# Paired rows of w_out per descriptor, gate and value weights read with a column step of two

## The chip, the cores and the metric

The kernel runs on one core of one Trainium2 chip. The metric is device time in microseconds of one execution. Before the change its median over 7 runs is 797.02 us (796.52 to 797.72).

## The reference

A light convolution over the sequence is followed by a gated feed-forward block. `x` is 8 x 4096 x 192, `weight` is 8 heads x 7 taps, `w_gate` and `w_val` are 192 x 1536 and `w_out` is 1536 x 192.

```
w = softmax(weight, axis=-1)                       # per head, 7 taps
x_pad = 6 zero rows ahead of each sequence
conv[b, s, h, :] = sum_k w[h, k] * x_pad[b, s + k, h, :]     # 24 columns a head
t = conv.reshape(32768, 192)
g = t @ w_gate;  v = t @ w_val
out = (g * sigmoid(g) * v) @ w_out                 # float32
```

## The kernel before

The 32768 tokens are cut into 64 blocks of 512 tokens. For each block the 1536 hidden columns are cut into 12 chunks of 128, so the main loop has 768 steps; step `n` is block `n // 12`, chunk `n % 12`. TensorE holds 192 = 3 x 64 input columns as three slices of 64 rows: the rows 0 to 63 of the array work on the gate and the rows 64 to 127 on the value, so one pair of matmuls (64 rows x 128 columns, 512 tokens) runs side by side. A step is three such pairs (L530), then ScalarE's Silu of the gate (L539) and VectorE's product with the value (L541), which gives `h` as 128 hidden columns x 512 tokens. `gate` and `val` have three PSUM banks each.

The hidden columns come from `w16`, the two weight matrices side by side in SBUF: 128 partitions x 3 x 1536, fp16. The stationary operand of chunk `j` is 128 neighbouring columns of it. The partition of `h` is therefore the hidden column within the chunk, and `wo16[p, j, :]` has to hold the row of `w_out` that belongs to it.

The down-projections (`slot`, `down`, L556) are put between the steps, four slots a block, each of 12 to 36 matmuls of 64 rows x 192 columns, in pairs again. Which slot stands behind which step is written out by hand in the loop from L645 on. For the first block it has its own numbers (slots at n = 9, 11, 13); from the second block on the slots stand at j = 1, 4, 7, 10. `after` is the Silu whose end a slot waits for.

The convolution is a product with a band matrix, made on the chip. Its taps are normalised (softmax), split into two fp16 numbers (`split`), brought onto the partitions by two matmuls (`tapbank`, L279), spread along 16 columns (`spread`, L290) and multiplied with shifted unit matrices (`shift`, L234) into `taps` (L310), four pieces of 16 columns. Four copies make `wide` of them (L323). The first four blocks are convolved on their own path: `early(e)` multiplies `wide` with the windows `xe[e]` of x (L365), casts it into `tme` (L383), and, for the blocks 0 to 2, `eturn` transposes it on TensorE (L423) with the unit matrix `ident` (L331) and copies it into `xc` (L428). The block 3 goes through memory (`eout`, `efetch`). From the second unit of four blocks on, `conv_half` does the same with larger windows in `x16`, and its result goes through memory and a transposing transfer.

Each engine works in the order in which the instructions are written (`seq`). GpSimd's queue issues all loads that change the type: `xe`, `w16` (`load_w`, three transfers a piece, in pieces of 384, 640 and 512 columns), `wo16` (`load_wo`, two halves), then the later `xe` and `x16`. Between them stand its iotas: `pid` and `jn` at the head, `cid` (L194) behind the third piece of `w16`. `ident` compares `cid` with `pf`. `keep_warm` gives TensorE matmuls on zeros ahead of the taps' products, so that it isn't idle there: seven of 512 columns, and, behind the products into `tapbank`, five of 128.

Of the kernel before, what the change touches and what calls it, by code (L numbers as in the profile page):

```python
# [10 lines left out]
def kernel(  # L11
# [9 lines left out]
    nc = tc.nc  # L21
    fp32 = mybir.dt.float32
    fp16 = mybir.dt.float16
    i32 = mybir.dt.int32
# [10 lines left out]
    P = 128  # L35
# [78 lines left out]
    def xe_load(e):  # L114
        for r, (g0, g1) in enumerate(ER):
            w0, w1 = 2 * g0, 2 * g1
            if e == 0 and r == 0:
                windows(xe[e], 0, 0, EO, 1, w1)
                windows(xe[e], 0, 0, EO, 0, 1, i0=pad, i1=Q - 2)
            else:  # L120
                windows(xe[e], Q * r, e * TB, EO, w0, w1, at=w0)

# [47 lines left out]
    def load_wo(c0, c1):  # L170
        seq(
            nc.gpsimd.dma_start(
                out=wo16[:, c0:c1, :],
                in_=moe_w_out[P * c0 : P * c1, :].rearrange("(c p) d -> p c d", p=P),
            )
        )

# [2 lines left out]

    pid = small("pid", [P, 1], i32)
    seq(nc.gpsimd.iota(pid, pattern=[[0, 1]], base=0, channel_multiplier=1))
    jn = small("jn", [P, 4, Q], i32)
    seq(nc.gpsimd.iota(jn, pattern=[[-16, 4], [1, Q]], base=0, channel_multiplier=0))  # L184
    xe_tile(0)
    seq(nc.vector.memset(xe[0][0:Q, 0, :], 0.0))
    xe_load(0)
    load_w(0, 384)
    load_w(384, 1024)
    xe_tile(1)  # L190
    xe_load(1)
    load_w(1024, Dff)
    cid = small("cid", [P, P], i32)
    seq(nc.gpsimd.iota(cid, pattern=[[1, P]], base=0, channel_multiplier=0))  # L194
    load_wo(0, 6)
    load_wo(6, NCH)
    xe_tile(2)
# [4 lines left out]
    for r in range(2):  # L202
        for low in (0, 32):
            load_x(1, r, low=low)

    pq_i = small("pq_i", [P, 1], i32)
    seq(nc.vector.tensor_single_scalar(pq_i, pid, 15, op=ALU.bitwise_and))
    pq = small("pq", [P, 1])
    seq(nc.vector.tensor_copy(pq, pq_i))
    pk = small("pk", [P, 1])  # L210
    seq(nc.vector.tensor_tensor(pk, pid, pq, op=ALU.subtract))
    eye = small("eye", [P, 16], fp16)
    seq(
        nc.vector.tensor_scalar(
            eye, jn[:, 0, 0:16], scalar1=pq, scalar2=None, op0=ALU.is_equal
        )
    )
    eyes = small("eyes", [P, 16, 2 * H], fp16)
    seq(nc.scalar.copy(eyes, eye.unsqueeze(2).to_broadcast([P, 16, 2 * H])))
    both = small("both", [P, 1])  # L220
    seq(
        nc.vector.scalar_tensor_tensor(
            both, pk, 1.0 / 16, pq, op0=ALU.mult, op1=ALU.add
        )
    )
    wexp = small("wexp", [H, K + 1])
    seq(nc.vector.memset(wexp[:, K : K + 1], 1e-9))
    split = small("split", [H, 2, K + 1, 16], fp16)
    seq(nc.vector.memset(split[:, :, K, :], 0.0))
    shift = small("shift", [P, 4, 2, Q], fp16)  # L230

    def make_shift(n):
        seq(
            nc.vector.tensor_tensor(  # L234
                shift[:, n : n + 2],
                jn[:, n : n + 2].unsqueeze(2).to_broadcast([P, 2, 2, Q]),
                both.unsqueeze(2).unsqueeze(3).to_broadcast([P, 2, 2, Q]),
                op=ALU.is_equal,
            )
        )  # L240

    make_shift(0)

    wmax = small("wmax", [H, 1])
    seq(nc.vector.tensor_reduce(wmax, wraw, axis=AX.X, op=ALU.max, negate=True))
    seq(nc.scalar.activation(wexp[:, 0:K], wraw, AF.Exp, bias=wmax))
    warmed = small("warmed", [P, 1], fp16)
    seq(nc.scalar.activation(warmed, fill[:, 0:1], AF.Silu))
    make_shift(2)
    wsum = small("wsum", [H, 1])  # L250
    seq(nc.vector.tensor_reduce(wsum, wexp, axis=AX.X, op=ALU.add))
    seq(nc.vector.reciprocal(wsum, wsum))
    wide_exp = wexp[:, 0:K].unsqueeze(2).to_broadcast([H, K, 16])
    seq(
        nc.vector.tensor_tensor(
            split[:, 0, 0:K],
            wide_exp,
            wsum.unsqueeze(2).to_broadcast([H, K, 16]),
            op=ALU.mult,
        )  # L260
    )
    seq(
        nc.vector.scalar_tensor_tensor(
            split[:, 1, 0:K],
            wide_exp,
            wsum,
            split[:, 0, 0:K],
            op0=ALU.mult,
            op1=ALU.subtract,
        )  # L270
    )
    tap = small("tap", [P, 2 * H], fp16)
    spread = small("spread", [P, 16, 2, H], fp16)

    def spread_taps():
        bank = apool.tile([P, TB], fp32, tag="acc0", name="tapbank")
        for a in range(2):
            seq(
                nc.tensor.matmul(  # L279
                    bank[:, a * H : a * H + H],  # L280
                    split[:, a].rearrange("h k q -> h (k q)"),
                    eye[0:H, 0:H],
                    start=(a == 0),
                    stop=True,
                    skip_group_check=True,
                )
            )
        seq(nc.vector.tensor_copy(tap, bank[:, 0 : 2 * H]))
        seq(
            nc.vector.tensor_tensor(  # L290
                spread.rearrange("p j a h -> p j (a h)"),
                eyes,
                tap.unsqueeze(1).to_broadcast([P, 16, 2 * H]),
                op=ALU.mult,
            )
        )

    wide = small("wide", [P, 2, H, Q], fp16)
    band = small("band", [P, H, 32], fp16)
# [3 lines left out]
    def make_wide():  # L303
        banks = [
            ppool.tile([P, TB], fp32, tag=tag, name="taps") for tag in ("gate", "val")
        ]
        for n in range(4):
            c0 = 16 * 2 * H * (n % 2)
            seq(
                nc.tensor.matmul(  # L310
                    banks[n // 2][:, c0 : c0 + 16 * 2 * H],
                    shift[:, n].rearrange("p r i -> p (r i)"),
                    spread.rearrange("p j a h -> p (j a h)"),
                    start=(n % 2 == 0),
                    stop=True,
                    skip_group_check=True,
                )
            )
        seq(nc.vector.tensor_copy(pf, pid))
        for h0 in (0, 4):  # L320
            for n in range(2):
                seq(
                    (nc.scalar.copy, nc.vector.tensor_copy)[n](  # L323
                        wide[:, :, h0 : h0 + 4, 32 * n : 32 * n + 32],
                        banks[n].rearrange("p (j a h) -> p a h j", a=2, h=H)[
                            :, :, h0 : h0 + 4, :
                        ],
                    )
                )
        seq(  # L330
            nc.vector.tensor_scalar(  # L331
                ident, cid, scalar1=pf, scalar2=None, op0=ALU.is_equal
            )
        )

# [186 lines left out]
    def gate_val(n):  # L522
        b, j = divmod(n, NCH)
        g = ppool.tile([P, TB], fp32, tag="gate", name="gate")
        v = ppool.tile([P, TB], fp32, tag="val", name="val")
        for k in range(SL):
            for half, o in ((0, g), (1, v)):
                p0 = Q * half
                seq(
                    nc.tensor.matmul(  # L530
                        o,
                        w16[p0 : p0 + Q, k, ts(j, P)],
                        xc[b][k][p0 : p0 + Q, 0:TB],
                        start=(k == 0),
                        stop=(k == SL - 1),
                    )
                )
        sg = hpool.tile([P, TB], fp16, tag="sig", name="sig", bufs=3)
        silu[n] = seq(nc.scalar.activation(sg, g, AF.Silu)).ins  # L539
        hj = hpool.tile([P, TB], fp16, tag="h", name="h", bufs=15)  # L540
        seq(nc.vector.tensor_tensor(hj, sg, v, op=ALU.mult))  # L541
        hbuf[n] = hj
# [79 lines left out]

    warm = ppool.tile([P, TB], fp32, tag="gate", name="warm")

    def keep_warm(count, width=TB):
        for _ in range(count):
            seq(
                nc.tensor.matmul(  # L628
                    warm[:, 0:width], fill[:, 0:P], fill[:, 0:width],
                    start=True, stop=True, skip_group_check=True,  # L630
                )
            )

# [1 line left out]
    acc_banks = (apool, "acc0"), (apool, "acc1")  # L635
    keep_warm(7)
    spread_taps()
    keep_warm(5, P)
    make_wide()
    early(0, (gate_bank, gate_bank, val_bank))  # L640
    eturn(0, (*acc_banks, gate_bank))
# [3 lines left out]
    for n in range(n_steps):  # L645
        b, j = divmod(n, NCH)
        u, ls = divmod(n, ustep)
        work = None
        if n in (11, 19):

            def work(e=2 if n == 11 else 3):
                early(e, (gate_bank, gate_bank, val_bank))

        at = (28, 31) if u == 0 else (10, 22)
# [3 lines left out]
                conv_half(u + 1, hh)  # L658

        gate_val(n)  # L660
        if n == 5:
            early(1, (*acc_banks, gate_bank))
        elif n == 7:
            eturn(1, (*acc_banks, gate_bank))
        elif n in (9, 11):
            slot(1 if n == 9 else 2, b, silu[n - 1], work)
        elif n == 13:
            slot(3, 0, silu[n - 1])
        elif j % 3 == 1 and b:
            k = {1: 3, 4: 4, 7: 1, 10: 2}[j]  # L670
            slot(k, b - 1 if j < 7 else b, silu[n - 2], work if j > 4 else None)
            if j == 4 and work:
                work()
        if n == 18:
            eturn(2, (*acc_banks, gate_bank))
        elif n == 20:
            eout(3)
        elif n == 21:
            efetch(3)
        if u + 1 < NU:  # L680
            if ls == at[0]:
                conv_dup(u + 1)
# [59 lines left out]
```

## Time and profile before

| | before |
|---|---|
| median of 7 runs | 797.02 us (796.52 to 797.72) |
| the profiled execution's own time | 797.6 us |
| its span in the profile | 795.8 us |
| TensorE matmuls busy | 785.1 us (99%) |
| VectorE busy | 583.1 us (73%) |
| ScalarE busy | 522.0 us (66%) |
| gate and value matmuls (L530) | 4608 of 377 ns, their loads 94 ns |
| down-projection matmuls (L556) | 6096 of 243 ns, their loads 94 ns |
| first gate matmul starts at | 12.47 us |

The span is from the first instruction to the last; the 1.8 us between span and time lie around it. Matmuls are pipelined: one of 512 columns is in flight for 377 ns, but in the steady state the next pair starts about 215 ns after the last, so the mean duration isn't the price of a matmul. PEld are the loads of the stationary operand, which run beside the matmuls. The granted clock of TensorE was 0.994 over the whole span; it is below 1 between 8.4 and 15.2 us and again at the end.

### The profile page before, as it was taken

How to read it: one execution, taken by the hardware profiler on the slowest of the kernel's cores; microseconds unless marked ns; L12 is line 12 of the kernel's file. 1: busy time of each engine (PE TensorE's matmuls, PEld its weight loads, DVE VectorE, ACT ScalarE, POOL GpSimd, SP SyncE). 2: the span in 40 equal slices, each digit the busy share in tenths (PEclk: the TensorE clock that was granted, in tenths of full speed). 3: DMA queues.
4: the chain of work that ended last, by engine and by line, in shares of the span. 5: the costliest groups of instructions: out<-in, count | busy, mean ns of one | idle time of the engine just before them, and what ended most of it. 6: DMA issues, size and time to landing. Idle time of an engine off the chain costs nothing.

```text
span 795.8 us, 28566 instructions
## 1 busy us (share of the span) xinstructions
PE 785.1 (99%) x12007; PEld 496.8 (62%) x12007; DVE 583.1 (73%) x928; ACT 522.0 (66%) x910; POOL 67.7 (9%) x94
## 2 busy tenths in 40 slices
PE   7999999999999999999999999999999999999997
PEld 3666666666676666666666666666666666666664
DVE  5777768777777777777778687687777777777775
ACT  5666766667666666666666666666666666666664
POOL 8010001010100101001010010100001010000000
PEclk8999999999999999999999999999999999999999
DMA  9999677795757859579694777858479783725311
GB/s 142 130 183 144 127 134 117 156 138 123 120 104 160 125 141 119 116 148 128 139 140 103 128 121 160 135 123 126 99 157 124 151 134 100 142 75 119 77 42 42
DMA packets 214961, 99.22 MB, mean 125 GB/s; under 512 B 148776, under 2 KB 213936, under 8 KB 213936
## 3 DMA queue, kind: packets, MB, share of 16 engines
q1 hardware_dynamic: 167424, 78.75, 48.3%
q0 software_dynamic: 47136, 18.45, 21.0%
q8 instruction: 94, 1.54, 0.8%
q14 instruction: 35, 0.29, 0.1%
q10 hardware_dynamic: 272, 0.20, 0.1%
HBM read 36.89 MB, written 41.16 MB: 98 GB/s over the span
## 4 chain that ended last, share of the span: by engine, by line
PE 98%; POOL 1%; DVE 0%; ACT 0%; issue 0%; POOLq 0%
PE gate L530 61%; PE acc L556 32%; PE cv L454 2%; PE val L530 2%; POOL w L162 1%; PE turn L423 0%; POOL xe L97 0%; PE acc L577 0%; PE cv L365 0%; DVE h L541 0%; ACT sig L539 0%; DVE tm L471 0%; ACT o_sb L710 0%; DVE o_sb L612 0%; POOL jn L184 0%
## 5 line engine op out<-in xcount | busy, mean ns | idle before, releaser
L541 DVE TENSOR_TENSOR h<-sig,val 128x512 f16<-128x512 f16 x768 | 507.9, 688 | 196.8 <-PE val L530 189.9
L539 ACT ACTIVATE sig<-gate 128x512 f16<-128x512 f32 x768 | 458.5, 597 | 237.0 <-PE val L530 207.6
L530 PE MATMUL val<-xc,w 64*128 64x512 f16 x2304 | 540.3, 377 | 0.2 <-DVE tm L471 0.2
L530 PE MATMUL gate<-xc,w 64*128 64x512 f16 x2304 | 540.3, 377 | 0.0
L530 PEld LDWEIGHTS <-w 64*128 64x128 f16 x4608 | 223.3, 94 | 211.9 <-issue 2.7
L556 PE MATMUL acc<-wo,h 64*128 64x192 f16 x6096 | 299.4, 243 | 0.4 <-issue 0.3
L556 PEld LDWEIGHTS <-h 64*128 64x128 f16 x6096 | 258.0, 94 | 66.9 <-issue 6.6
L97 POOL DMA_DIRECT2D x<-in_x_dram x40 | 31.6, 793 | 441.5 <-ACT sig L539 433.9
L471 ACT CAST tm<-cv 128x480 f16<-128x480 f32 x60 | 30.6, 562 | 22.1 <-PE cv L454 22.1
L471 DVE CAST tm<-cv 128x480 f16<-128x480 f32 x60 | 36.7, 652 | 2.6
L612 DVE COPY o_sb<-acc 128x384 f32<-128x384 f32 x63 | 34.7, 550 | 0.0
L482 POOL COPY tm<-tm 128x1280 f16<-128x1280 f16 x15 | 18.8, 1253 | 137.7 <-DVE tm L471 110.0
L611 ACT COPY o_sb<-acc 128x384 f32<-128x384 f32 x63 | 30.1, 478 | 0.0
L454 PE MATMUL cv<-x,band 64*32 64x240 f16 x960 | 18.2, 265 | 0.0
L454 PEld LDWEIGHTS <-band 64*32 64x32 f16 x960 | 10.1, 91 | 4.9 <-issue 4.7
L423 PE MATMUL turn<-ident,tme 128*128 128x128 f16 x45 | 4.0, 249 | 3.5 <-DVE ident L331 3.5
L132 POOL MEMSET x<- 6x192 f16 x7 | 1.7, 248 | 59.7 <-PE cv L454 59.6
L423 PEld LDWEIGHTS <-tme 128*128 128x128 f16 x45 | 3.2, 111 | 4.6 <-issue 3.8
L97 POOL DMA_DIRECT2D xe<-in_x_dram x9 | 6.0, 695 | 0.1
L628 PE MATMUL warm<-fill 128*128 128x512 f16 (+1 forms) x12 | 3.8, 492 | 1.2 <-DVE fill L91 1.2
L428 ACT COPY xc<-turn 128x520 f16<-128x520 f16 x3 | 1.8, 592 | 4.7 <-PE turn L423 4.5
L383 ACT CAST tme<-cv 128x288 f16<-128x288 f32 x8 | 2.9, 401 | 2.1 <-PE cv L365 2.1
(52 smaller groups left out, 38.6 us busy)
## 6 DMA issues: line engine op xcount, KB each, us to landing
out_dram<-o_sb SPq DMA_DIRECT2D x63, 384.0 KB
scr<-tm SPq DMA_DIRECT2D x105, 130.0 KB
x<-x SPq DMA_DIRECT2D x28, 480.0 KB
x<-in_x_dram POOLq DMA_DIRECT2D x24, 480.0 KB, 9.6
x<-in_x_dram POOLq DMA_DIRECT2D x7, 468.0 KB, 7.4
xc<-scr SPq DMA_TRANSPOSE x180
scr<-tm SPq DMA_DIRECT2D x15, 104.0 KB
wo<-in_moe_w_out_dram POOLq DMA_DIRECT2D x2, 288.0 KB, 6.6
```

The source lines that it names most:

```text
L97: nc.gpsimd.dma_start(out=t[p0 + i0 : p0 + i1, w0 - at : w1 - at, :], in_=bass.AP(tensor=x_flat.tensor, offset=(t0 + size * w0 - pad + i0) ...
L162: nc.gpsimd.dma_start(out=w16[Q * half : Q * half + Q, i0:i1, f0:f1], in_=src[Q * s0 : Q * (s0 + i1 - i0), f0:f1].rearrange("(s q) f -> q ...
L423: nc.tensor.transpose(bank[:, g, :], tme[b][:, g, Q * k : Q * k + P], ident)
L454: nc.tensor.matmul(banks[r][32 * c : 32 * c + 32, t * w : t * w + w], band[Q * r : Q * r + Q, h, :], x16[u][Q * r : Q * r + Q, NG * c : NG ...
L471: eng(tm[u][:, NG * r : NG * r + NG, 2 * grp * hp : 2 * grp * hp + 2 * grp].rearrange("p g (t e) -> p g t e", t=2), banks[r][:, 0 : 2 * w] ...
L482: seq(nc.gpsimd.tensor_copy(tm[u][:, :, SL * Q : 4 * Q], tm[u][:, :, 0:Q]))
L530: nc.tensor.matmul(o, w16[p0 : p0 + Q, k, ts(j, P)], xc[b][k][p0 : p0 + Q, 0:TB], start=(k == 0), stop=(k == SL - 1),)
L539: silu[n] = seq(nc.scalar.activation(sg, g, AF.Silu)).ins
L541: seq(nc.vector.tensor_tensor(hj, sg, v, op=ALU.mult))
L556: nc.tensor.matmul(acc[b][bank][:, s, :], hj[p0 : p0 + Q, ts(2 * bank + s, P)], wo16[p0 : p0 + Q, j, :], start=(not second and j == 0 and ...
L611: seq(nc.scalar.copy(o_sb[:, 0:2, :], acc[b][0]))
L612: seq(nc.vector.tensor_copy(o_sb[:, 2:4, :], acc[b][1]))
```

## The change

It changes five things.

- `w_out` is loaded with two neighbouring rows per partition and descriptor: partition `p` of the chunks 2m and 2m + 1 holds the rows 256 m + 2p and 256 m + 2p + 1. So that `h` fits to it, the gate and value weights of chunk `j` are every second column of 256: the stationary operand of L530 has a column step of two.
- The pieces of `w16` are 512, 512 and 512 columns in place of 384, 640 and 512.
- The band comes from two pieces of 32 columns. The taps are brought onto the partitions by 16 small matmuls (8 x 32, 8 columns) in place of 2, `spread` is made in two operations of 512 elements in place of one of 256, and four products of 512 columns, added up in pairs, take the place of four of 256. `shift` is made in four operations in place of two, and `split` is 8 x 7 in place of 8 x 112.
- One iota `jid` at the head of GpSimd's queue, cast to `jf`, serves `eye`, `shift` and `ident`; the iotas `jn` and `cid` go.
- The first block's order: `early(1)` behind n = 4 (was 5), its transposes behind n = 6 (was 7), slots 1 and 2 at n = 7 and 10 (were 9 and 11) with `early(2)` in the latter, the transposes of block 2 behind n = 17 (was 18). The slots wait for `silu[n - 2]` everywhere. `keep_warm` is two matmuls of 512 columns behind the taps' products in place of five of 128. The first window of `xe[0]` is issued ahead of the others, and with 58 rows in place of 56.

```diff
             if e == 0 and r == 0:
+                windows(xe[e], 0, 0, EO, 0, 1, i0=pad)
                 windows(xe[e], 0, 0, EO, 1, w1)
-                windows(xe[e], 0, 0, EO, 0, 1, i0=pad, i1=Q - 2)
...
     def load_wo(c0, c1):
         seq(
             nc.gpsimd.dma_start(
-                out=wo16[:, c0:c1, :],
-                in_=moe_w_out[P * c0 : P * c1, :].rearrange("(c p) d -> p c d", p=P),
+                out=wo16[:, c0:c1, :].rearrange("p (m e) d -> p m (e d)", e=2),
+                in_=moe_w_out[P * c0 : P * c1, :].rearrange(
+                    "(m p e) d -> p m (e d)", p=P, e=2
+                ),
...
-    jn = small("jn", [P, 4, Q], i32)
-    seq(nc.gpsimd.iota(jn, pattern=[[-16, 4], [1, Q]], base=0, channel_multiplier=0))
+    jid = small("jid", [P, P], i32)
+    seq(nc.gpsimd.iota(jid, pattern=[[1, P]], base=0, channel_multiplier=0))
     xe_tile(0)
-    seq(nc.vector.memset(xe[0][0:Q, 0, :], 0.0))
+    seq(nc.vector.memset(xe[0][0:pad, 0, :], 0.0))
     xe_load(0)
-    load_w(0, 384)
-    load_w(384, 1024)
+    load_w(0, 512)
+    load_w(512, 1024)
...
     load_w(1024, Dff)
-    cid = small("cid", [P, P], i32)
-    seq(nc.gpsimd.iota(cid, pattern=[[1, P]], base=0, channel_multiplier=0))
...
+    tap = small("tap", [P, 2, 2, H], fp16)
+    spread = small("spread", [P, 2, 32, 2, H], fp16)
...
+        for i in range(2):
+            for a in range(2):
+                c0 = (2 * i + a) * H
+                for d in range(4):
+                    k = 4 * i + d
+                    seq(
+                        nc.tensor.matmul(
+                            bank[32 * d : 32 * d + 32, c0 : c0 + H],
+                            split[:, a, k : k + 1].to_broadcast([H, 32]),
+                            eye[0:H, 0:H],
...
+                            tile_position=(0, 32 * d),
...
+        for i in range(2):
+            for n in range(2):
+                seq(
+                    nc.tensor.matmul(
+                        banks[n],
+                        shift[:, n, i].rearrange("p r i -> p (r i)"),
+                        spread[:, i].rearrange("p j a h -> p (j a h)"),
+                        start=(i == 0),
+                        stop=(i == 1),
...
-                ident, cid, scalar1=pf, scalar2=None, op0=ALU.is_equal
+                ident, jf, scalar1=pf, scalar2=None, op0=ALU.is_equal
...
+        cols = 2 * P * (j // 2) + j % 2
...
-                        w16[p0 : p0 + Q, k, ts(j, P)],
+                        w16[p0 : p0 + Q, k, cols : cols + 2 * P - 1 : 2],
...
-    keep_warm(5, P)
+    keep_warm(2)
...
-        if n in (11, 19):
+        if n == 4:
+            def work():
+                early(1, (*acc_banks, gate_bank))
+        elif n in (10, 19):
...
+        if j % 3 == 1:
+            after = silu[n - 2] if n >= 2 else None
+            if j == 1:
+                if b:
+                    slot(3, b - 1, after)
+            elif j == 4:
+                if b:
+                    slot(4, b - 1, after)
+                if work:
+                    work()
+            else:
+                slot(1 if j == 7 else 2, b, after, work)
+        if u == 0:
+            if ls == 6:
+                eturn(1, (*acc_banks, gate_bank))
+            if ls == 17:
+                eturn(2, (*acc_banks, gate_bank))
```

More of the change, by code (lines that the diff above doesn't have):

```diff
@@ L204 @@
             load_x(1, r, low=low)
[L206 to L212, printed above, removed]
+    pm_i = small("pm_i", [P, 1], i32)
+    seq(nc.vector.tensor_single_scalar(pm_i, pid, 31, op=ALU.bitwise_and))
+    pm = small("pm", [P, 1])
@@ L213 @@
+    seq(nc.vector.tensor_copy(pm, pm_i))
+    jf = small("jf", [P, P])
+    seq(nc.vector.tensor_copy(jf, jid))
+    p32 = small("p32", [P, 1])
+    seq(nc.vector.tensor_tensor(p32, pid, pm, op=ALU.subtract))
+    pd = small("pd", [P, 1])
+    eye = small("eye", [P, 32], fp16)
     seq(
         nc.vector.tensor_scalar(
-            eye, jn[:, 0, 0:16], scalar1=pq, scalar2=None, op0=ALU.is_equal
+            eye, jf[:, 0:32], scalar1=pm, scalar2=None, op0=ALU.is_equal
         )
     )
-    eyes = small("eyes", [P, 16, 2 * H], fp16)
@@ L219 @@
-    seq(nc.scalar.copy(eyes, eye.unsqueeze(2).to_broadcast([P, 16, 2 * H])))
+    seq(
+        nc.vector.tensor_scalar(pd, p32, scalar1=1.0 / 32, scalar2=None, op0=ALU.mult)
+    )
     both = small("both", [P, 1])
-    seq(
-        nc.vector.scalar_tensor_tensor(
-            both, pk, 1.0 / 16, pq, op0=ALU.mult, op1=ALU.add
-        )
-    )
+    seq(nc.vector.tensor_tensor(both, pm, pd, op=ALU.add))
+    eyes = small("eyes", [P, 32, 2, H], fp16)
+    seq(
+        nc.scalar.copy(
+            eyes.rearrange("p j a h -> p j (a h)"),
+            eye.unsqueeze(2).to_broadcast([P, 32, 2 * H]),
+        )
+    )
@@ L226, with make_shift @@
+    shift = small("shift", [P, 2, 2, 2, Q], fp16)
+    def make_shift(n, i):
+        seq(
+            nc.vector.tensor_scalar(
+                shift[:, n, i],
+                jf[:, 0:Q].unsqueeze(1).to_broadcast([P, 2, Q]),
+                scalar1=both, scalar2=32.0 * n + 4.0 * i,
+                op0=ALU.subtract, op1=ALU.is_equal,
+            )
+        )
     wexp = small("wexp", [H, K + 1])
     seq(nc.vector.memset(wexp[:, K : K + 1], 1e-9))
-    split = small("split", [H, 2, K + 1, 16], fp16)
@@ L229 @@
[L229 to L242, printed above, removed]
+    split = small("split", [H, 2, K + 1], fp16)
+    seq(nc.vector.memset(split, 0.0))
@@ L244 @@
+    make_shift(0, 0)
+    make_shift(1, 0)
     wmax = small("wmax", [H, 1])
@@ L248 @@
     seq(nc.scalar.activation(warmed, fill[:, 0:1], AF.Silu))
-    make_shift(2)
+    make_shift(0, 1)
     wsum = small("wsum", [H, 1])
@@ L252 @@
     seq(nc.vector.reciprocal(wsum, wsum))
-    wide_exp = wexp[:, 0:K].unsqueeze(2).to_broadcast([H, K, 16])
     seq(
[L255 to L259, printed above, removed]
+        nc.vector.tensor_scalar(
+            split[:, 0, 0:K], wexp[:, 0:K], scalar1=wsum, scalar2=None, op0=ALU.mult
         )
@@ L264 @@
             split[:, 1, 0:K],
-            wide_exp,
+            wexp[:, 0:K],
             wsum,
@@ L271 @@
     )
-    tap = small("tap", [P, 2 * H], fp16)
-    spread = small("spread", [P, 16, 2, H], fp16)
+    make_shift(1, 1)
+    tap = small("tap", [P, 2, 2, H], fp16)
+    spread = small("spread", [P, 2, 32, 2, H], fp16)
     def spread_taps():
         bank = apool.tile([P, TB], fp32, tag="acc0", name="tapbank")
-        for a in range(2):
-            seq(
[L279 to L285, printed above, removed]
-                )
-            )
[L288 to L296, printed above, removed]
+        for i in range(2):
[3 more added lines that the diff above has]
+                    k = 4 * i + d
+                    seq(
+                        nc.tensor.matmul(
+                            bank[32 * d : 32 * d + 32, c0 : c0 + H],
+                            split[:, a, k : k + 1].to_broadcast([H, 32]),
+                            eye[0:H, 0:H],
+                            start=(c0 == 0),
+                            stop=True,
+                            skip_group_check=True,
+                            tile_position=(0, 32 * d),
+                        )
+                    )
+        seq(
+            nc.vector.tensor_copy(
+                tap.rearrange("p i a h -> p (i a h)"), bank[:, 0 : 4 * H]
+            )
+        )
+        for i in range(2):
+            seq(
+                nc.vector.tensor_tensor(
+                    spread[:, i].rearrange("p j a h -> p j (a h)"),
+                    eyes.rearrange("p j a h -> p j (a h)"),
+                    tap[:, i]
+                    .rearrange("p a h -> p (a h)")
+                    .unsqueeze(1)
+                    .to_broadcast([P, 32, 2 * H]),
+                    op=ALU.mult,
+                )
+            )
     wide = small("wide", [P, 2, H, Q], fp16)
@@ L306, in make_wide @@
         ]
[L307 to L316, printed above, removed]
+        for i in range(2):
+            for n in range(2):
+                seq(
+                    nc.tensor.matmul(
[4 more added lines that the diff above has]
+                        stop=(i == 1),
+                    )
                 )
-            )
         seq(nc.vector.tensor_copy(pf, pid))
@@ L623, with keep_warm @@
     warm = ppool.tile([P, TB], fp32, tag="gate", name="warm")
-    def keep_warm(count, width=TB):
+    def keep_warm(count):
         for _ in range(count):
@@ L628, in keep_warm @@
                 nc.tensor.matmul(
-                    warm[:, 0:width], fill[:, 0:P], fill[:, 0:width],
-                    start=True, stop=True, skip_group_check=True,
+                    warm, fill[:, 0:P], fill, start=True, stop=True,
+                    skip_group_check=True,
                 )
@@ L648, with work @@
         work = None
-        if n in (11, 19):
-            def work(e=2 if n == 11 else 3):
+        if n == 4:
+            def work():
+                early(1, (*acc_banks, gate_bank))
+        elif n in (10, 19):
+            def work(e=2 if n == 10 else 3):
                 early(e, (gate_bank, gate_bank, val_bank))
@@ L660 @@
         gate_val(n)
[L661 to L679, printed above, removed]
+        if j % 3 == 1:
[15 more added lines that the diff above has]
+                eturn(2, (*acc_banks, gate_bank))
+            if ls == 20:
+                eout(3)
+            if ls == 21:
+                efetch(3)
         if u + 1 < NU:
```

## The prediction

> **What bounds the kernel now.** I read the page first, then the granted clock by stretches, then the waits and the timeline of the first 13 us, then the groups by shape, and last the timeline near the end, for what stands between two kinds of matmul. The page:
>
> ```profile
> span 795.8 us, 28566 instructions
> PE 785.1 (99%) x12007; PEld 496.8 (62%) x12007; DVE 583.1 (73%) x928; ACT 522.0 (66%) x910; POOL 67.7 (9%) x94
> PE 98%; POOL 1%; DVE 0%; ACT 0%; issue 0%; POOLq 0%
> ```
>
> TensorE is busy for 785.1 of 795.8 us and the chain that ended last runs over it. Nothing in the main loop can be gained by an earlier transfer or a shorter VectorE operation; only TensorE's own work counts there. What is not TensorE's work is 10.7 us, of which about 5 us lie at the end (its last matmul ends near 791). The rest lies in the start:
>
> ```profile
> 6.00:7.50 1.50, 0.83 (x64) 0.73 (x64) 0.50 (x2) 0.91 (x3) 1.50 (x3) 1.00 1.11 131
> 7.50:10.60 3.10, 0.00 (x0) 0.10 (x1) 0.33 (x2) 0.04 (x1) 2.82 (x7) 0.64 1.10 164
> 10.60:12.50 1.90, 1.89 (x17) 1.43 (x17) 1.11 (x3) 0.46 (x1) 1.90 (x3) 0.50 1.44 191
> 12.50:15.00 2.50, 2.50 (x13) 1.06 (x14) 0.83 (x2) 0.73 (x2) 2.50 (x5) 0.50 1.38 193
> 15.00:18.00 3.00, 3.00 (x26) 1.15 (x22) 2.41 (x5) 2.43 (x5) 2.31 (x3) 0.97 1.60 189
> ```
>
> The columns are the stretch in us, its length, busy time of PE, PEld, DVE, ACT and POOL, the granted clock, the DMA share and GB/s. Between 7.5 and 10.6 us TensorE does nothing, and the clock falls to a half. 0.64 over 3.1 us is full clock until 8.35; 0.97 over 15 to 18 is half clock until 15.2. So the kernel pays twice: for the hole, and for 12.47 (first gate matmul) to 15.2 at half speed, which is 1.35 us of work. Who makes the hole is in the waits and the timeline:
>
> ```profile
> DVE ident L331 <- POOL cid L194: 3.8, 1, 3.8
> PE turn L423 <- DVE ident L331: 3.5, 1, 3.5
> ...
> 9.91 0.33 POOL L194 IOTA cid<- 128x128 int32 x1
> 10.27 0.29 DVE L331 TENSOR_SCALAR ident<-cid,pf 128x128 f16<-128x128 int32 x1 [3.77 <-POOL cid L194]
> 10.47 0.55 DVE L383 CAST tme<-cv 128x384 f16<-128x384 f32 x1
> 10.61 1.93 PE L423 MATMUL turn<-ident,tme 128*128 128x128 f16 x15 [3.52 <-DVE ident L331]
> ```
>
> The `cid` iota stands in GpSimd's queue behind the issues of fourteen transfers, at 9.91. VectorE works in order, so `ident` waits for it, and the `tme` cast behind `ident`, ready to run since about 7.2, waits too; the 15 transposes of the first block wait for both.
>
> **The change, part by part.** Sums are against the profiled execution (span 795.8, the run 797.6), and the difference is then taken from the median 797.02.
>
> *The hole.* `cid` is gone. `ident` reads `jf`, made from an iota that takes the place of `jn` (337 ns, `cid` 328) as GpSimd's second instruction. So `ident` is done right after the `wide` copies and the cast behind it is free. What is late next is the chain that makes `wide`, which the change makes longer. Before: products into `tapbank` at 4.30, `tap` 4.55, `spread` 4.76, the product `taps` 5.11, VectorE's `wide` copy 5.74, `early(0)` 6.27.
> - 16 matmuls into `tapbank` for 2. Bounds: 64 small matmuls of L365 take 0.83 us, 13 ns each, so 0.2 us; one after the other at the 172 ns of the row L279, 2.75 us. Four neighbours write four different column strips as those of L365 do, so I take 0.4 us more.
> - `spread` is two operations of 512 elements for one of 256 (291 ns): about 560 ns each. The products of the first run under the second, so +0.85 us. Behind it two products of 512 columns, about 0.6 us, as the four of 256 were (0.60 us).
> - The VectorE operations before `split` are more in number but smaller (`split` 8x7 for 8x112, 322 and 262 ns before); they end near 4.0, under the seven `warm` matmuls that run to 4.3. If that cover were gone, each costs its 150 ns.
>
> `early(0)` then starts at 6.27 + 0.4 + 0.85 = 7.5 and takes 0.83; the DVE cast (0.55) and copy (0.26) with gaps of 0.1 end near 9.4; the last five transposes take 0.3 us at full clock or 0.65 at half (a third of the 0.94 of the next block's transposes, at full clock, and of the 1.93 here). First gate matmul: 10.0 (9.7 to 10.6) in place of 12.47. **2.5 us.**
>
> *Is the data there?* The first piece of `w` grows from 384 to 512 columns, 96 KB more ahead of the first matmul. Before, its last transfer was issued at 4.6 and landed 4.0 us later, at 8.7; at the 164 to 193 GB/s of these stretches 96 KB is 0.5 to 0.6 us: 9.2, and at most 10.3, when the whole second piece had begun to land (issue 5.16 + 5.1). Covered by 0.8 us; uncovered it costs 0.3. The first window of `xe` is loaded whole (58 rows for 56) and first; it is wanted at 7.5 rather than 6.27, so the longer chain covers it. Two rows per descriptor for `w_out`: the queue carries 189 GB/s in 15 to 18 us with single rows and 191 to 193 with the longer rows of `w`, so I book nothing, and `w_out`'s first half lands near 17 as before (10.51 + 6.3).
>
> *Clock.* In the trace the clock fell 1.2 us after the last matmul of `early(0)` (7.10) and rose 4.6 us after the transposes began. After the change the hole is about 1 us at 8.4 to 9.4 with few transposes in it, and the stretch before holds more work (products of 2048 columns instead of 1024). Ends: 0, if the clock falls and stays half for as much matmul work as before, and 1.35, if it never falls. I take the middle, **0.7 us**. [...]
>
> *What comes early.* `early(1)`, its transposes and the first two down-projections move up by one or two steps (n = 5, 7, 9, 11 to 4, 6, 7, 10). The PE work is the same. But at full clock a step takes TensorE 0.65 us and VectorE 0.69 (h, 688 ns), and 0.81 us of casts come among the first seven; three PSUM banks absorb two steps. The slot at n = 7 would stand at 10.0 + 8 x 0.65 + 0.66 + 0.94 = 16.8, as `w_out` lands. Cost 0 to 1.0, taken **0.4 us**, since both waits end at the same place and don't add.
>
> *The weight load with a column step of two.* 4608 loads of 64x128. No row of the trace has a stationary operand with a step.
>
> ```profile
> L530 PEld LDWEIGHTS <-w 64*128 64x128 f16 x4608 | 223.3, 94 | 211.9 <-issue 2.7
> ...
> L454 PEld LDWEIGHTS <-band 64*32 64x32 f16 x960 | 10.1, 91 | 4.9 <-issue 4.7
> ...
> L365 PEld LDWEIGHTS <-wide 64*64 64x64 f16 x256 | 2.6, 107 | 1.6 <-ACT wide L323 0.8 <-issue 0.7
> ...
> 784.07 1.15 PE L556 MATMUL acc<-wo,h 64*128 64x192 f16 x24
> 784.98 1.69 PEld L530 LDWEIGHTS <-w 64*128 64x128 f16 x18
> 785.06 0.38 PE L530 MATMUL gate<-xc,w 64*128 64x512 f16 x1
> ```
>
> Between gate and val pairs a load has 215 ns (783.21 to 783.42 and on); even one lengthened by half stays hidden. After a down-projection it has only the last pair there, 784.98 to 785.06: 82 ns for a load of 94, so there is no slack, and every ns more is paid, four times a block, some 254 times. Ends: 0, because 32 columns (91) and 128 columns (94) cost the same now, so the step may be hidden in the fixed part; and a load that goes column by column: 16 ns per 32 columns (107 less 91), 91 + 3 x 16 = 139, 45 ns more, 254 x 45 = 11.4 us. A gain is excluded, since the columns are as many. I take 0: the four columns' worth of work of 128 against 32 shows that the load isn't bound by its columns.
>
> [...]
>
> Sum: 2.5 + 0.7 - 0.4 = 2.8 us, span 793.0, the run **794.2**, 0.35% below 797.02. About 0.2% (1.6 us) is what a measurement here tells from no change.
>
> **The rivals.**
> - *A, the forecast* (0.67): 794.2, its own range 792.9 (clock term 1.35, gate at 9.7, no wait) to 796.1 (no clock term, gate at 10.6, a wait of 1.0).
> [...]
> - *C, the strided load goes column by column* (0.12), the slower side: 254 x 45 = 11.4 us, 805.6; if the two loads of a pair also queue behind each other, twice that, 817. It decides from 11 ns per slot end (2.8 / 254) on, and is over the measurable bound from 17.
> - *D, the start gains nothing* (0.11): the 16 tap products run one after the other (2.5 us) and TensorE only finds its hole in another place, earlier; 796.5 to 797.5, up to 799 if the first `w` lands late as well.
>
> **How the numbers follow.** Faster by over 0.2%: nearly all of A, 0.61. Within: the weak end of A 0.06, half of B 0.05, most of D 0.07: 0.18. Slower: C 0.12, the other half of B 0.05, the rest of D 0.04: 0.21. The range 792.4 to 798.6 holds A (with the 0.5 us by which the runs before lie under their median), D and over half of B; C is left out.
>
> **What would show it.** Right: no wait of `ident` for GpSimd; the first gate matmul between 9.7 and 10.6; `early(0)` near 7.5; loads of L530's successor at 94 to 100 ns and the gate matmul still 80 to 85 ns behind its load after a down-projection; from 40 us on the same busy time per us. Wrong in the start: `tapbank` products of over 1 us, or a wait of the first gate matmul on `w`. Wrong in the main loop: loads of 110 ns or more, and 200 us stretches that hold fewer matmuls than before.

## The result, and the profile after

The changed kernel takes 799.72 us (median of 13 runs, 798.33 to 800.55) against 797.37 (33 runs, 796.29 to 798.27). The ratio is 1.0028, 95% interval 1.0021 to 1.0036: slower by 0.28%, a little over the 0.2% that the prediction gave as the least that a measurement here tells. The forecast was 794.2, with 792.4 to 798.6 as its range: wrong in sign. The profiled execution took 800.01 us, its span is 798.2.

The page of the changed kernel: span, the chain by line, and two groups (line, engine, what it writes and reads, busy us, mean ns, idle before and who ended it).

```profile
span 798.2 us, 28592 instructions
...
PE gate L548 61%; PE acc L574 32%; PE cv L471 2%; PE val L548 2%; DMA w<-in_moe_w_val_dram 1%; POOL w L162 1%; POOL xe L97 0%; PE acc L595 0%; PE cv L382 0%; PE turn L440 0%; DVE h L559 0%; ACT sig L557 0%; DVE o_sb L630 0%; DVE tm L488 0%; ACT o_sb L734 0%
...
L548 PE MATMUL gate<-xc,w 64*128 64x512 f16 x2304 | 541.7, 377 | 4.5 <-DMA w<-in_moe_w_gate_dram 4.5
...
L548 PEld LDWEIGHTS <-w 64*128 64x128 f16 x4608 | 221.5, 94 | 219.4 <-DMA w<-in_moe_w_gate_dram 4.8
```

Two things are there at once. The strided weight load still takes 94 ns. And one gate matmul waits 4.5 us for a transfer of `w`, which is new: a transfer of the value weights now stands in the chain that ended last. The stretches of the start, columns as before (us, length, PE, PEld, DVE, ACT, POOL, clock, DMA share, GB/s):

```profile
7.50:10.60 3.10, 2.10 (x81) 1.54 (x76) 1.97 (x6) 1.36 (x3) 2.52 (x5) 1.00 1.11 162
10.60:12.50 1.90, 0.00 (x0) 0.00 (x0) 0.00 (x0) 0.00 (x0) 1.56 (x3) 1.00 1.42 190
12.50:15.00 2.50, 0.44 (x1) 0.10 (x1) 0.00 (x0) 0.00 (x0) 2.17 (x4) 0.60 1.24 182
15.00:18.00 3.00, 2.84 (x15) 1.01 (x16) 0.80 (x2) 1.19 (x2) 2.85 (x4) 0.50 1.35 185
18.00:22.00 4.00, 4.00 (x89) 1.77 (x87) 2.77 (x5) 2.49 (x5) 2.78 (x7) 0.77 1.58 189
```

The hole between 7.5 and 10.6 us is filled, and a longer one stands behind it: TensorE, VectorE and ScalarE idle from 10.6 to 12.5 (GpSimd goes on issuing transfers), and TensorE up to 14.56. The clock goes to a half during it (at 13.0 by the trace's clock records) and comes back at 19.8. The timeline of the start (start, length, engine, line, operation, and what ended the idle time before it):

```profile
7.37 0.83 PE L382 MATMUL cv<-xe,wide 64*64 64x72 f16 x64 [0.56 <-ACT wide L340]
...
8.52 0.63 POOL L162 DMA_DIRECT2D w<-in_moe_w_gate_dram  x1 [0.27 <-DMA w<-in_moe_w_gate_dram]
...
8.70 1.04 PE L440 MATMUL turn<-ident,tme 128*128 128x128 f16 x15 [0.50 <-ACT tme L400]
...
9.18 1.14 POOL L162 DMA_DIRECT2D w<-in_moe_w_val_dram  x2
...
9.70 0.37 PE L548 MATMUL gate<-xc,w 64*128 64x512 f16 x1
9.70 0.39 PE L548 MATMUL val<-xc,w 64*128 64x512 f16 x1
...
14.56 0.61 PE L548 MATMUL gate<-xc,w 64*128 64x512 f16 x1 [4.47 <-DMA w<-in_moe_w_gate_dram]
...
15.33 0.61 PE L548 MATMUL val<-xc,w 64*128 64x512 f16 x1 [0.16 <-DMA w<-in_moe_w_val_dram]
```

`early(0)` starts at 7.37 and the first pair at 9.70, as forecast (7.5, 10.0). Then the second pair of the very first step, slice k = 1 of chunk 0, waits. The columns that it reads are in the first piece of `w16`, and by the trace's landing records the three transfers of that piece had landed by 8.24, 8.89 and 9.26 us. The chain names what it waited for:

```profile
9.18 6.11 DMA w<-in_moe_w_val_dram
15.33 0.61 PE val L548
```

A transfer issued at 9.18 is one of the *third* piece, columns 1024 to 1535, which no matmul needs before step 8. Its gate transfer (issued at 8.52) landed at 14.51 and its first value transfer at 15.28: the two instants at which the gate and the value matmul of k = 1 go on. The semaphore waits of the two programs say the same (the points at which an instruction is held until a transfer has landed; they are put in when the program is built). For the first weight loads of step 0, the transfers on which each waits (g and v: gate and value, 1 to 3: the piece):

```
read (half, slice)    before             changed
gate, k = 0           g1                 g1
val,  k = 0           v1                 v1
gate, k = 1           none more          g2, g3
val,  k = 1           none more          v2, v3
```

The reads of k = 1 lie within the first piece; the program makes TensorE wait for all three.

### The profile page after: what moved, and what is told of

The parts are those of the page before. It is cut to its first block, busy times and chain, and to the rows that moved or that the text cites. A ratio compares the mean times of both kernels' runs of the same rounds, so it can differ in the third digit from the quotient of the medians.

```text
span 798.2 us, 28592 instructions
## 1 busy us (share of the span) xinstructions
PE 786.1 (98%) x12018; PEld 494.3 (62%) x12018; DVE 584.0 (73%) x933; ACT 522.2 (65%) x910; POOL 67.3 (8%) x93
## 4 chain that ended last, share of the span: by engine, by line
PE 97%; POOL 1%; DMA 1%; DVE 0%; ACT 0%; issue 0%; POOLq 0%
PE gate L548 61%; PE acc L574 32%; PE cv L471 2%; PE val L548 2%; DMA w<-in_moe_w_val_dram 1%; POOL w L162 1%; POOL xe L97 0%; PE acc L595 0%; PE cv L382 0%; PE turn L440 0%; DVE h L559 0%; ACT sig L557 0%; DVE o_sb L630 0%; DVE tm L488 0%; ACT o_sb L734 0%
## 5 line engine op out<-in xcount | busy, mean ns | idle before, releaser
L646 PE MATMUL warm<-fill 128*128 128x512 f16 x9 | 4.2, 626 | 1.2 <-DVE fill L91 1.2
L382 PEld LDWEIGHTS <-wide 64*64 64x64 f16 x256 | 2.6, 107 | 1.8 <-ACT wide L340 1.0
```

## The experiments

Theory 1: the program's dependencies, not the data, stop TensorE; a stepped read (every second column) is taken to collide with the other pieces' transfers, that is, to need what they write. Rival 2: the data is late, since the first piece is a third longer. Rival 3: the strided load itself costs. Each of the nine kernels was timed beside the kernel before, on the same chip within a group; the ratios are against that group's median of it: 796.85 for the first four, 797.23 for the next three, 797.04 for the last two.

**Three tensors.** The changed kernel; each piece of `w16` is a tensor of its own (`WP` is 512), and `cols` counts within the piece.

```diff
-    w16 = wpool.tile([P, SL, Dff], fp16, tag="w16", name="w16")
+    w16 = [
+        wpool.tile([P, SL, WP], fp16, tag=f"w16{i}", name=f"w16{i}") for i in range(3)
+    ]
...
-                    out=w16[Q * half : Q * half + Q, i0:i1, f0:f1],
+                    out=w16[f0 // WP][Q * half : Q * half + Q, i0:i1, :],
...
-        cols = 2 * P * (j // 2) + j % 2
+        cols = 2 * P * (j % 4 // 2) + j % 2
...
-                        w16[p0 : p0 + Q, k, cols : cols + 2 * P - 1 : 2],
+                        w16[j // 4][p0 : p0 + Q, k, cols : cols + 2 * P - 1 : 2],
```

> The changed kernel with w16 cut into three tensors of 512 columns, one for each piece of the load; the step of two stays. Theory 1 (the program's wait of the first k = 1 gate load covers the second and third piece too, though its columns came with the first): each weight load can wait only for its own piece, the 4.5 us wait at 9.7 us is gone, the gate matmuls run on from 9.7; 5.3 us less by the wait, 0 to 2.2 us less by the clock, 0.4 us more because VectorE is then the slower one: 793.2 us, 792 to 795. Rival 2 (the data itself is late, because the first piece is a third longer): the wait stays, 799 to 800.5. Rival 3 (the strided load is what costs): the main loop does not change, 797 to 800.

Measured: 793.40 us (793.07 to 793.74) against 796.85, ratio 0.9953 (0.9941 to 0.9966). The timeline of TensorE in it:

```profile
10.22 0.37 PE L551 MATMUL gate<-xc,w 64*128 64x512 f16 x1
10.22 0.39 PE L551 MATMUL val<-xc,w 64*128 64x512 f16 x1
10.66 0.37 PE L551 MATMUL gate<-xc,w 64*128 64x512 f16 x1
...
10.66 0.39 PE L551 MATMUL val<-xc,w 64*128 64x512 f16 x1
10.87 0.38 PE L551 MATMUL gate<-xc,w 64*128 64x512 f16 x1
```

No wait on `w` is left, although the transfers and their sizes are the same. Rival 2 falls.

**The step alone.** The kernel before with the step of two, the paired rows and three pieces of 512 columns.

```diff
+        cols = 2 * P * (j // 2) + j % 2
...
-                        w16[p0 : p0 + Q, k, ts(j, P)],
+                        w16[p0 : p0 + Q, k, cols : cols + 2 * P - 1 : 2],
...
-    load_w(0, 384)
-    load_w(384, 1024)
+    load_w(0, 512)
+    load_w(512, 1024)
...
-                in_=moe_w_out[P * c0 : P * c1, :].rearrange("(c p) d -> p c d", p=P),
+                in_=moe_w_out[P * c0 : P * c1, :].rearrange(
+                    "(m p e) d -> p m (e d)", p=P, e=2
+                ),
```

> The kernel before with only the column step of two, the paired rows of w_out and pieces of 512, 512 and 512 columns. Theory 1: the first gate matmul still starts at about 12.4, but the k = 1 pair then waits for the third piece, which lands at 13.7 to 14.7 (gate, value): 1.5 to 1.8 us more than before, 799.1 us, 798.3 to 800.5. Rival 2: at 12.4 the first piece is long there, so 797.4 within 0.5. Rival 3: the start is as before and 4 us or more are spread over the main loop, 801 or more.

Measured: 798.57 us (798.15 to 800.91) against 796.85, ratio 1.0025 (1.0014 to 1.0036). The timeline of its longest execution (800.91 us), the one that was profiled:

```profile
12.48 0.60 PE L533 MATMUL gate<-xc,w 64*128 64x512 f16 x1
...
14.04 0.60 PE L533 MATMUL gate<-xc,w 64*128 64x512 f16 x1 [0.95 <-DMA w<-in_moe_w_gate_dram]
14.76 0.60 PE L533 MATMUL val<-xc,w 64*128 64x512 f16 x1
```

The same false wait, shorter, because the old hole had used up most of the time that the third piece needs: the value matmul of k = 1 starts at 14.76 in place of 12.88. The name-giving part of the change, with its equal pieces, makes the kernel slower by about as much as the whole.

**The rest alone.** The changed kernel with neighbouring columns and single rows of `w_out` (the first and third hunk above, backwards).

> The changed kernel with neighbouring columns and single rows of w_out again: the change without its name-giving part. Theory 1: no wait on the third piece, the same as with three tensors within 0.5 us, 793.2 us, 792 to 795. Rival 2: pieces are as long as in the change, so the wait stays, 799 to 800.5. Rival 3: 4 us or more faster in the main loop, with the wait at 9.7 us still there, 795 to 796.

Measured: 793.37 us (793.00 to 794.53), ratio 0.9957 (0.9944 to 0.9969): the same as with three tensors. With the wait gone, the step of two and the pairs cost and bring nothing that shows. In the main loop the two profiles agree to the resolution: from the start of the 601st gate matmul to that of the last, 568.75 us with the step (three tensors) and 568.75 without. Rival 3 falls.

**cid first.** The kernel before with the iota of `cid` moved.

```diff
+    cid = small("cid", [P, P], i32)
+    seq(nc.gpsimd.iota(cid, pattern=[[1, P]], base=0, channel_multiplier=0))
     xe_tile(0)
...
     load_w(1024, Dff)
-    cid = small("cid", [P, P], i32)
-    seq(nc.gpsimd.iota(cid, pattern=[[1, P]], base=0, channel_multiplier=0))
```

> The kernel before with the iota of cid moved to the head of GpSimd's queue and nothing else: the hole alone. The prediction's reading of the hole: ident waits for nothing, the transposes start near 7.5 and end near 8.5, the first gate matmul starts near 9.0 (its piece of w lands at 8.7 to 9.1), 3.4 us less by the hole, 0 to 1.35 us less by the clock, up to 0.8 us more in waits for the second piece of w (it lands near 11.4): 793.5 us, 792.3 to 795. If the first piece of w were the true bound of the start: first gate matmul near 12, 797.

Measured: 793.08 us (792.76 to 795.20), ratio 0.9955 (0.9942 to 0.9969). The timeline (operations of VectorE and TensorE):

```profile
6.38 0.28 DVE L331 TENSOR_SCALAR ident<-cid,pf 128x128 f16<-128x128 int32 x1
...
7.56 1.77 PE L423 MATMUL turn<-ident,tme 128*128 128x128 f16 x15 [0.50 <-ACT tme L383]
...
9.26 0.61 PE L530 MATMUL gate<-xc,w 64*128 64x512 f16 x1
```

`ident` waits for nothing, and the first gate matmul stands 3.2 us earlier than before. So the hole was real, and this one move is worth about as much as the whole repaired change. In this profile the clock was half from 7.61 to 11.03 us; over the five runs the granted clock was 0.996 in the profiled one and 0.999 to 1.000 in the other four, so such a stretch is not there every time.

**Pieces outermost.** Why does the program see a collision? `w16` lies in each partition as three slices of 1536 columns. The gate transfer of the second piece writes 512 columns in each of three slices, from column 512 of slice 0 to column 1023 of slice 2; its span, all that lies between the first and the last column written, has the columns 0 to 511 of the slices 1 and 2 inside it, though it doesn't write them. (The first value transfer does the same over the slices 0 and 1.) This kernel has one tensor again, but the pieces lie one behind the other.

```diff
-    w16 = wpool.tile([P, SL, Dff], fp16, tag="w16", name="w16")
+    w16 = wpool.tile([P, 3, SL, WP], fp16, tag="w16", name="w16")
...
-                    out=w16[Q * half : Q * half + Q, i0:i1, f0:f1],
+                    out=w16[Q * half : Q * half + Q, f0 // WP, i0:i1, :],
...
-        cols = 2 * P * (j // 2) + j % 2
+        cols = 2 * P * (j % 4 // 2) + j % 2
...
-                        w16[p0 : p0 + Q, k, cols : cols + 2 * P - 1 : 2],
+                        w16[p0 : p0 + Q, j // 4, k, cols : cols + 2 * P - 1 : 2],
```

> The changed kernel with w16 as one tensor again, but laid out by pieces: partition x piece x slice x 512 columns, in place of slice x 1536 columns. Same transfers, same bytes, same step of two. Theory 1a (the program takes a stepped read and a transfer to collide when their spans within the partition overlap, and the second and third pieces, each spread over three slices, span the first piece's slices 1 and 2): the pieces now span separate stretches, no wait but for the own piece, the same as with three tensors: 793.4 us, 792.6 to 794.5. Rival 1b (a stepped read waits for every load of its tensor that is issued before it): the wait for the third piece stays, now at the first pair already, 799 to 801.

Measured: 793.01 us (792.92 to 793.11) against 797.23, ratio 0.9948 (0.9934 to 0.9962). 1a holds and 1b falls: a stepped read is compared with a transfer by the spans of both. That also says why k = 0 was free in the changed kernel: its span, columns 0 to 254 of slice 0, ends before the second piece's begins. Reads with neighbouring columns out of the same single tensor (the kernel before and *the rest alone*) had no such wait. This kernel's median is the lowest of all, but not clear of *cid first* and the other repaired ones.

All four repaired kernels end near 793, though their first gate matmuls stand between 9.26 and 10.22. The chain of this kernel names a next bound (start, length, what):

```profile
7.54 6.05 DMA xe<-in_x_dram
13.64 0.72 PE cv L383 x59
```

`early(1)` waits for block 1's windows, which land at 13.6. Four more kernels went after that, the clock and the order, all built on *cid first*.

**Fills.** Two matmuls of 512 columns on zeros ahead of `early(0)` and two behind it (`fills`).

```diff
     make_wide()
+    idle = apool.tile([P, TB], fp32, tag="acc1", name="idle")
...
+    fills(2)
     early(0, (gate_bank, gate_bank, val_bank))
+    fills(2)
```

> The kernel before with cid first (793.1 us) and two matmuls on zeros of 512 columns before early(0) and two behind it, to fill TensorE's gaps at 5.7 and 7.1 us. If the clock falls because of these gaps (it was half from 7.6 to 11.0 in the profile of cid first): the clock stays full from the taps on, 0.9 us less, 792.2 us, 791.5 to 793. If the clock goes by something else: 793.1 to 794, since the fills can push the transposes back by up to 0.8 us.

Measured: 793.21 us (792.84 to 793.33), ratio 0.9949 (0.9937 to 0.9962). In the profile the clock stayed full from 4.48 to 789.5 us and the first gate matmul moved to 8.77, but nothing came of it:

```profile
13.96 0.19 PE L365 MATMUL cv<-xe,wide 64*64 64x72 f16 x1 [0.69 <-DMA xe<-in_x_dram]
14.32 0.72 PE L365 MATMUL cv<-xe,wide 64*64 64x48 f16 x63 [0.18 <-DMA xe<-in_x_dram]
```

TensorE gets there earlier and waits 0.87 us for the windows. The expectation missed: it had not looked at what is late next. Nor is it shown that the fills held the clock. The next two kernels have none, and in their profiles it stayed full from 4.63 and 5.14 us on, with the first gate matmul at 8.77 and 8.79; four of the five runs of *cid first* itself were at 0.999 or more.

**The changed kernel's order.** *cid first* with the loop order of the change (`early(1)` behind n = 4, slots at n = 7 and 10).

> The kernel before with cid first and the changed kernel's order of the first block (early(1) behind n = 4, slots at n = 7 and 10). The prediction's reading: TensorE's work is the same, and the earlier slots cost 0 to 1 us of waits for h and w_out: 793.1 to 794.1 us. If the earlier order relieves VectorE in the first ten steps instead: 792.3 to 793.

Measured: 793.98 us (793.42 to 795.88), ratio 0.9965 (0.9952 to 0.9977); its interval overlaps that of *cid first*, so a cost of the order between 0 and 1 us is neither shown nor excluded.

**Block 1 later.** *cid first* with `early(1)` behind n = 7 and its transposes behind n = 9, without and with the fills.

```diff
-        if n == 5:
+        if n == 7:
             early(1, (*acc_banks, gate_bank))
-        elif n == 7:
+        elif n == 9:
             eturn(1, (*acc_banks, gate_bank))
-        elif n in (9, 11):
+        if n in (9, 11):
```

> The kernel before with cid first, and early(1) behind n = 7 in place of 5, its transposes behind n = 9 in place of 7. Theory 4 (once the hole is gone the start is bound by the landing of block 1's windows at 13.6 to 14.3, which early(1) needs): two more steps of block 0 run before they are wanted, no wait for xe; at full clock 0.9 us less than cid first with fills (793.2), at half clock until 11.0 about as much as cid first: 792.2 to 793.1. Rival (the first steps are bound by VectorE's 0.69 us a step or by the second piece of w): no gain, 793.0 to 793.5.

> The same with the four matmuls on zeros around early(0), which held the clock at full. Theory 4: the clock's 0.9 us now shows, since no transfer stands behind it: 792.2 us, 791.6 to 792.8, and less than without the fills. Rival: 793.0 to 793.5, no difference between the two.

Measured: 794.06 us (792.79 to 794.63), ratio 0.9959 (0.9945 to 0.9973), and 793.32 us (793.07 to 793.75), ratio 0.9951 (0.9939 to 0.9964). The wait for the windows is gone in both, and no time with it; the two intervals overlap, so a difference between them isn't shown. TensorE and VectorE of the one with fills:

```profile
12.58 3.35 DVE L541 TENSOR_TENSOR h<-sig,val 128x512 f16<-128x512 f16 x5 [0.46 <-PE gate L530]
...
18.13 0.76 DVE L428 COPY xc<-turn 128x520 f16<-128x520 f16 x2
...
18.41 1.34 PE L556 MATMUL acc<-wo,h 64*128 64x192 f16 x24 [0.40 <-ACT xc L428]
```

Now the first slot waits for the copies out of the transposes, whose PSUM banks it needs. Theory 4 is not borne out: the windows are not the only bound there. That VectorE's pace is the one behind them is likely (back-to-back `h` at 0.67 us), but no run here separated it.

## Why the prediction was wrong

*The failing step is "Is the data there?".* It worked out when the first piece lands, 9.2, which the trace confirms (9.26), and called the wait covered by 0.8 us. It took for granted that a matmul waits for the transfer that brings its columns and for no other; among its signs of being wrong stood a wait of the first gate matmul on `w`, but only as late data. The step of two changed what the program takes for a collision, and the wait was put on the third piece, 15.28. The price, 4.47 us of idle TensorE ahead of the second pair, was not a term of the sum at all. In the two profiles TensorE's continuous run starts at 15.33 in place of 12.88, 2.45 us later, and the half clock afterwards lasts 4.5 us in place of 2.3, another 1.1 us; 3.5 together, of which 3.1 is left where the second unit's convolution starts (49.22 against 46.10). In that one pair of executions the main loop then gives 0.6 back; the spans differ by 2.4, and the medians by 2.35. Taking the wait away and nothing else (*three tensors*, *pieces outermost*) brings the ratio from 1.0028 to 0.9953 and 0.9948, some 6 us.

*Two questions were treated as one.* The part on the strided load asked only how long the load takes. Its answer was right: 94 ns in 4608 loads, and after a down-projection the gate matmul still follows 80 ns behind its load, with the step:

```profile
787.51 1.48 PEld L548 LDWEIGHTS <-w 64*128 64x128 f16 x16
787.59 0.38 PE L548 MATMUL gate<-xc,w 64*128 64x512 f16 x1
```

Rival C's 139 ns did not come. No run shows B, to which the chances give 0.10, a load that the step slows to some 110 ns: the loads took 94 ns with it as without it. The slower side came from a mechanism that was in none of the rivals. D named the place, a hole that TensorE finds elsewhere and a late `w`, but with another cause and at 799 at most.

*The rest of the sum.* The hole and its cause were right: *cid first* shows them alone, 3.8 us by its medians. The longer chain was priced at +1.25 us; `early(0)` at 7.37 in place of 6.27 is +1.1, with the second `spread` cheaper (both in 0.76 us, not 1.12) and the products partly at half clock (1.39 us). The 16 products into `tapbank` took 0.35 us where the 2 had taken 0.21, so +0.14 and not the +0.4 booked. Paired rows of `w_out` brought nothing that shows, as booked. Without the false wait the forecast of the time stands: 794.2 against 793.4, 793.4 and 793.0 in the three kernels that keep the rest of the change. Part of that is luck: the sum booked 0.7 us for the clock, the middle between 0 and 1.35, and in the profiles of these three the clock was full from before the first gate matmul until near the end, the upper bound's case. Its price is smaller than that bound, it seems: of the runs of the kernel before beside the experiments, five had a granted clock of 0.998 or more, with a median of 796.4 us against 797.3 for the other 24; they are few, and the times overlap. The sum had not seen that the clock also decides when the chain ends: as it rose at 4.45, 6.15, 7.02 and 7.23 us (*pieces outermost*, the changed kernel, *the rest alone*, *three tensors*), the four `taps` products took 1.02, 1.39, 1.82 and 1.90 us and the first gate matmul stood at 9.33, 9.70, 10.20 and 10.22. The 0.4 for what comes early was not measured by itself. What is late next turned out to be the windows of block 1, which the sum had not looked at; an earlier start than these ran into them (*fills*).

## What to carry to other kernels

Before booking an earlier start, ask what each consumer will *wait* for, not only what it reads: a stepped access pattern on a tensor that arrives in pieces can be tied to all of them, as here, where the second pair waited 4.47 us for the third piece. If a tensor arrives in pieces, lay it out so that each piece's span is its own, as separate tensors or with the piece as the outermost dimension; that costs no instruction and here gave 0.75% (three tensors) and 0.8% (pieces outermost) over the kernel as it was changed. And when a large hole closes, look for the next late thing at once: here starts at 8.77, 9.26 and 10.22 us (*fills*, *cid first*, *three tensors*) ended between 793.1 and 793.4.

## What the runs showed of the hardware

- A weight load of 64x128 with a column step of two fp16 costs nothing that shows here: 94 ns each, 568.75 us for the same stretch of the main loop with and without it.
- The changes of the clock lay 3.41 us or twice that apart in the start of two profiles. By the trace's clock records it was full at 4.94, half at 8.35 and full at 15.18 in the kernel before; full at 6.15, half at 12.98, full at 19.81 in the changed one. The views count full clock ahead of the first record, but the 512-column matmuls on zeros there took 631 ns each in the kernel before, as long as its gate matmuls at half clock (0.63 us from 12.87 to 14.58). In the kernel before it fell 1.25 us after the last matmul of `early(0)`, and in *cid first* at 7.61, while transposes ran and with no idle stretch of TensorE over 0.6 us since 4.2. What makes it fall, no run here shows. In *three tensors* it rose only at 7.23 and then stayed full to 788.9.
- In two profiles one of the sixteen parts of a transfer lagged: block 1's first windows in *fills* had fifteen landed by 12.30 and the last at 13.91 us. The matmul that waited for it started at 13.96, behind that last part. Of the third gate transfer in the changed kernel fifteen had landed by 13.98 and the last at 14.51; the gate matmul went on at 14.56.
